# Twenty-four weight-sum stores move from SyncE's DMA queue to GpSimd's beside the first MoE's paired blocks

## The chip, the cores and the metric

The kernel runs on one core of one Trainium2 chip. The metric is the device time of one execution in microseconds (us), compared as the median of several runs. The engines are named as in the profile: PE (TensorE), DVE (VectorE), ACT (ScalarE), POOL (GpSimd) and SP (SyncE, which only issues DMAs here). "SPq" is SP's sequencer.

## The reference, cut to what matters

Three stages follow one another over 3072 tokens of width 512: chunked attention with memory tokens, a gated MLP ("MoE 1", d_ff 1536) and a second MLP ("MoE 2", d_ff 2048). Weights and activations are float32.

```python
def _moe_ref(x, w_gate, w_val, w_out, rms_g):
    rms = np.sqrt(np.mean(x * x, axis=-1, keepdims=True) + 1e-06)
    xn = x / rms * rms_g
    g = xn @ w_gate
    silu = g * (1.0 / (1.0 + np.exp(-g)))
    return (silu * (xn @ w_val) @ w_out).astype(np.float32)

def _moe2_ref(x, w_in, w_out):
    h = x @ w_in
    g = np.where(h >= 1.0, h, np.where(h <= -1.0, 0.0, (h + 1.0) ** 2 / 4.0))
    return (g @ w_out).astype(np.float32)
```

## The kernel before, in words

A float32 product is made of three fp32r matmuls (high x high, high x low, low x high), so every operand is split into a high part (an ACT copy to fp32r) and a low part (a DVE subtraction).

The six token tiles of 512 are treated in two ways. The first four go through MoE 1 one at a time (the "single" part, up to about 487 us), while attention for the later tiles runs in between. The last two go through MoE 1 together as a pair, and then MoE 2 takes all six tiles as three pairs. For a pair, a 2x2 block product is done with 7 products of sub-blocks instead of 8 (Strassen's scheme, in `seven`). That needs, beside the raw weight blocks, four sums and differences of weight blocks for each group of weights. These are prepared once, in the background, split into high and low parts, and stored to DRAM in `w1p_d`, `w1o_d` (MoE 1) and `w2p_d`, `w2o_d` (MoE 2), from where the pair stages load them again.

The background work is a list of small steps, `bg`, taken off by `conv_step`. For MoE 2, `w2_steps(g)` handles one group of four weight blocks in 28 steps:

- `load_w2` loads a raw 512 KB block `w` through POOL's queue (line 274). It takes one of three buffers, so it waits until an earlier block's stores have landed.
- `c`, `join`, `hi`, `lo` turn the 64-bit words into float32 and split them (ACT line 287, DVE lines 144 and 145, ACT line 290, DVE line 293). `lo` stores the split blocks through POOL's queue (line 301).
- `pair_sums` makes two sums of two blocks (DVE lines 196 to 200). Then `hi_s` (ACT line 203) and `lo_s` (DVE line 206) split each, and `lo_s` stores the two parts with two DMAs of 256 KB each (line 208), all on SP's queue.

The sums stand in the tiles `late`, two of them in turn; the high part overwrites one of the float32 blocks (`tu` or `g_b`).

In the pair stage of MoE 1 the loop `for f in range(F1)` (12 blocks) calls `proj1`, and that calls `seven`: seven `product`s of 6 matmuls each. After product i, SP is told to load the weights of product i + 14 into the 14 slots of `wp` (part of the tile `wall`, line 807). Background steps are called between the products. ACT and DVE move the sums of products between the PSUM banks and make the activations.

The order of all instructions on all engines is written out by hand here (`manual_schedule`). Each engine takes its instructions in program order: a DMA that waits for its data holds up everything behind it on the same engine.

`m2["single"]` is true until the single part is over. It is set to False just before the pair stage of MoE 1, after the background sums in progress have been finished.

Of the kernel before, what the change touches and what calls it, by code (L numbers as in the profile page):

```python
# [39 lines left out]
def tile_stream_attention_moe_moe2(  # L40
# [10 lines left out]
    nc = tc.nc  # L51
# [153 lines left out]
    def lo_s(S, k, h, dst):  # L205
        tt_(out=flat(S[k]), in0=flat(S[k]), in1=h.bitcast(F32), op=ALU.subtract)
        for n, src in enumerate((h.bitcast(F32), flat(S[k]))):
            nc.sync.dma_start(dst(n, k), src.rearrange("p (k c) -> p k c", k=2))

    def in_dst(dp):  # L210
        return lambda n, k: dp[:, 3 + 2 * k:5 + 2 * k, n]
# [14 lines left out]
    def sum_steps(i, srcs, raws, order, dst):  # L226
        n = 8 * i
        h, S = [], []

        def whole():  # L230
            if i % 2:
                h.extend(tmp.tile([P, 512], U32, tag="tu", name="wgv") for _ in range(2))
            else:
                gv = wst.tile([P, 1024], U32, tag="w64", name="wgv")
                h.extend([gv[:, :512], gv[:, 512:]])
            for x, w in zip(h, srcs):
                tt_(out=x.bitcast(F32), in0=w[:, 0], in1=w[:, 1], op=ALU.add)

        def first():
            S.extend(halves(wst.tile([P, 1024], F32, tag="w64", name="s1234")))  # L240
            sums(S, *order(h), True)

        at(n, lambda: (nc.gpsimd.dma_start(*raws[0]), whole()))
        at(n + 1, first)
        at(n + 2, lambda: sums(S, *order(h), False))
        for k, r in enumerate(raws[1:]):
            at(n + 2 + 2 * k, lambda r=r: nc.gpsimd.dma_start(*r))
        at(n + 4, lambda: hi_s(S, 0, h[0]))
        at(n + 5, lambda: hi_s(S, 1, h[1]))
        at(n + 6, lambda: lo_s(S, 0, h[0], dst))  # L250
        at(n + 7, lambda: lo_s(S, 1, h[1], dst))
# [26 lines left out]
    def w2_steps(g):  # L278
# [38 lines left out]
        def pair_sums(a, b, n, order, dst):  # L317
            S, h = [], lambda: (f32_[a], f32_[b])

            def first():  # L320
                if m2["single"]:
                    S.extend([sp.tile([P, TT], F32, tag="s", name="s12"), sums_.tile([P, TT], F32, tag="s34", name="s34")])
                else:
                    S.extend(m2["late"][a // 2 % 2][:, i] for i in range(2))
                S[:] = [x.rearrange("p (k c) -> p k c", k=2) for x in S]
                live.append(a)
                sums(S, *order(h()), True)

            at(n + 10, first)
            at(n + 11, lambda: sums(S, *order(h()), False))  # L330
            at(n + 13, lambda: hi_s(S, 0, f32_[a]))
            at(n + 14, lambda: hi_s(S, 1, f32_[b]))
            at(n + 15, lambda: lo_s(S, 0, f32_[a], dst))
            at(n + 16, lambda: (lo_s(S, 1, f32_[b], dst), live.remove(a)))
# [4 lines left out]
    m2 = {"single": True, "pace": 0.0, "hold": False}  # L339
# [302 lines left out]
    for st in ORDER.split():  # L642
        c, n = st[0], st[1:]
# [3 lines left out]
        n = int(n)  # L647
# [26 lines left out]
        elif c == "L":  # L674
            dst, hi = (x[:, :, n * P:n * P + P] for x in (xl, xh))
# [631 lines left out]
```

## Time and profile before

| | us |
|---|---|
| median of 3 runs | 1133.96 |
| lowest and highest run | 1133.13, 1137.2 |
| the profiled execution's own time | 1134.45 |
| its span in the trace | 1132.7 |

The span runs from the first to the last instruction of the trace; the execution's own time holds 1.75 us more around it. Times in the trace count from the start of the span. The page gives busy time by engine; queries of the trace give it by stretch of time, and what each instruction waited for. The stretch that the change touches is the pair stage of MoE 1, from 486.9 to 601.2 us.

### The profile page before, as it was taken

The page shows a single profiled execution, that of the slowest core. Times are in us where ns is not written, and L with a number is a line of the kernel's source. Part 1 is how long each engine was busy: PE and PEld are TensorE (multiplying, and loading weights), DVE is VectorE, ACT ScalarE, POOL GpSimd, SP SyncE. Part 2 cuts the span into 40 slices and gives each one's busy share as a digit, 9 for nine tenths or more (in the row PEclk, how much of TensorE's full clock was granted, in tenths as well). Part 3 has the DMA queues.
Part 4 walks back from the last instruction along what each step waited for, and adds up shares of the span by engine and source line. Part 5 has one row for each costly group of instructions (what it writes and reads, how often), then busy time and mean ns, then how long its engine had stood idle before and what let it go on. Part 6 is the DMA issues. An engine that isn't in the chain of part 4 may idle for free.

```text
span 1132.7 us, 20941 instructions
## 1 busy us (share of the span) xinstructions
PE 1113.5 (98%) x7882; PEld 911.7 (80%) x7882; DVE 817.4 (72%) x1433; ACT 617.1 (54%) x1089; POOL 102.8 (9%) x152
## 2 busy tenths in 40 slices
PE   6999999999999999999999999999999999999998
PEld 4777888888888888788888888888888888888886
DVE  4987666777666766666767867897678987578855
ACT  3887655666567765534445544466344565344553
POOL 0200003221222122111110000000000000000000
PEclk6999999999999999999999999999999999999999
DMA  8967259998878976899997798756778666762564
GB/s 281 359 232 256 87 187 298 299 349 291 286 248 288 299 261 220 291 320 382 404 390 223 217 318 259 202 182 199 234 205 268 186 190 219 221 197 83 168 193 159
DMA packets 144212, 281.81 MB, mean 249 GB/s; under 512 B 15216, under 2 KB 65392, under 8 KB 142320
## 3 DMA queue, kind: packets, MB, share of 16 engines
q1 hardware_dynamic: 123936, 228.83, 62.3%
q0 software_dynamic: 12768, 43.52, 11.2%
q10 hardware_dynamic: 7408, 8.13, 2.1%
q8 instruction: 62, 1.02, 0.4%
q14 instruction: 38, 0.31, 0.1%
HBM read 201.26 MB, written 79.17 MB: 248 GB/s over the span
## 4 chain that ended last, share of the span: by engine, by line
PE 92%; DVE 3%; ACT 2%; DMA 1%; issue 1%; SPq 0%; POOL 0%; DVEq 0%; ACTq 0%; POOLq 0%
PE ps_y L1085 14%; PE ps_g L1085 11%; PE ps_g L567 7%; PE ps_g L569 7%; PE ps_g L568 7%; PE ps_b L903 4%; PE ps_b L905 4%; PE ps_b L904 4%; PE ps_g L903 4%; PE ps_g L905 4%; PE ps_g L904 4%; PE ps_y L567 4%; PE ps_y L569 3%; PE ps_y L568 3%; PE ps_y L903 2%; PE ps_y L905 2%
## 5 line engine op out<-in xcount | busy, mean ns | idle before, releaser
L1085 PE MATMUL ps_y<-r,wo 128*128 128x512 f32 x672 | 156.7, 391 | 0.0
L567 PE MATMUL ps_g<-xh,wall 128*128 128x512 f32 x380 | 151.8, 399 | 1.2 <-ACT s L866 0.7
L569 PE MATMUL ps_g<-xh,wall 128*128 128x512 f32 x380 | 148.5, 391 | 1.0 <-DVE wall L160 1.0
L568 PE MATMUL ps_g<-xl,wall 128*128 128x512 f32 x380 | 148.3, 390 | 0.0
L1085 PEld LDWEIGHTS ps_y<-r,wo 128*128 128x128 f32 x672 | 125.6, 188 | 26.6 <-DVE r L1024 0.8
L1024 DVE TENSOR_TENSOR r<-h,r 128x512 fp32r<-128x512 f32 x155 | 103.9, 689 | 44.3 <-ACT r L1022 44.3
L975 ACT ACTIVATE t<-t,half 128x512 f32<-128x512 f32 x96 | 66.9, 720 | 122.7 <-DVE t L974 122.7
L1022 ACT ACTIVATE r<-h 128x512 fp32r<-128x512 f32 x155 | 93.1, 625 | 56.2 <-DVE r L1024 17.5
L1085 PE MATMUL ps_g<-r,wo 128*128 128x512 f32 x498 | 116.0, 390 | 0.0
L1085 PEld LDWEIGHTS ps_g<-r,wo 128*128 128x128 f32 x498 | 93.2, 188 | 19.3 <-DVE r L1024 0.2
L567 PEld LDWEIGHTS ps_g<-xh,wall 128*128 128x128 f32 x380 | 71.3, 188 | 17.9 <-ACT s L866 1.2
L569 PEld LDWEIGHTS ps_g<-xh,wall 128*128 128x128 f32 x380 | 71.4, 188 | 16.5 <-DVE wall L160 1.4
L568 PEld LDWEIGHTS ps_g<-xl,wall 128*128 128x128 f32 x380 | 71.4, 188 | 13.8
L903 PE MATMUL ps_b<-wall 128*128 128x512 f32 x202 | 78.8, 390 | 0.0
L905 PE MATMUL ps_b<-wall 128*128 128x512 f32 x202 | 78.7, 390 | 0.0
L904 PE MATMUL ps_b<-wall 128*128 128x512 f32 x202 | 78.7, 389 | 0.0
L903 PE MATMUL ps_g<-wall 128*128 128x512 f32 x198 | 77.4, 391 | 0.0
L905 PE MATMUL ps_g<-wall 128*128 128x512 f32 x198 | 77.1, 390 | 0.0
L904 PE MATMUL ps_g<-wall 128*128 128x512 f32 x198 | 77.1, 390 | 0.0
L567 PE MATMUL ps_y<-hh,wall 128*128 128x512 f32 x192 | 76.7, 399 | 0.0
L568 PE MATMUL ps_y<-hl,wall 128*128 128x512 f32 x192 | 75.1, 391 | 0.0
L569 PE MATMUL ps_y<-hh,wall 128*128 128x512 f32 x192 | 75.0, 391 | 0.0
(209 smaller groups left out, 2101.9 us busy)
## 6 DMA issues: line engine op xcount, KB each, us to landing
wo<-w2o_d SPq DMA_DIRECT2D x88, 512.0 KB, 3.5
wall<-w2p_d SPq DMA_DIRECT2D x168, 256.0 KB, 3.1
wall<-w1p_d SPq DMA_DIRECT2D x84, 256.0 KB, 6.3
w<-in_w_dram POOLq DMA_DIRECT2D x32, 512.0 KB, 5.6
w<-in_w_dram SPq DMA_DIRECT2D x30, 512.0 KB, 5.2
k_in<-in_k_dram SPq DMA_DIRECT2D x48, 256.0 KB, 5.1
wo<-w1o_d SPq DMA_DIRECT2D x21, 512.0 KB, 3.7
v_in<-in_v_dram SPq DMA_DIRECT2D x40, 260.0 KB, 5.1
```

The source lines that it names most:

```text
L567: nc.tensor.matmul(ps, wh, xh, start=start, stop=False)
L568: nc.tensor.matmul(ps, wh, xl, start=False, stop=False)
L569: nc.tensor.matmul(ps, wl, xh, start=False, stop=stop)
L903: nc.tensor.matmul(bank, wh, xh, start=st, stop=False, skip_group_check=True)
L904: nc.tensor.matmul(bank, wh, xl, start=False, stop=False, skip_group_check=True)
L905: nc.tensor.matmul(bank, wl, xh, start=False, stop=kk == 1, skip_group_check=True)
L975: nc.scalar.activation(s, s, AF.Square, scale=0.5, bias=half)
L1022: nc.scalar.activation(r[:, 0], src, AF.Copy)
L1024: tt_(out=r[:, 1], in0=src, in1=r[:, 0].bitcast(F32), op=ALU.subtract)
L1085: nc.tensor.matmul(bank[p][m], a, b, start=s0, stop=s1, skip_group_check=True)
```

## The change

`lo_s`, which stores the parts of a weight sum, chooses its queue: SP while `m2["single"]` is true, as before, and GpSimd afterwards. Everything else stays as it was, so the stores of line 208 that fall in the pair stage of MoE 1 are issued by POOL, and SP's queue holds loads only there.

```diff
     def lo_s(S, k, h, dst):
         tt_(out=flat(S[k]), in0=flat(S[k]), in1=h.bitcast(F32), op=ALU.subtract)
         for n, src in enumerate((h.bitcast(F32), flat(S[k]))):
-            nc.sync.dma_start(dst(n, k), src.rearrange("p (k c) -> p k c", k=2))
+            queue = nc.sync if m2["single"] else nc.gpsimd
+            queue.dma_start(dst(n, k), src.rearrange("p (k c) -> p k c", k=2))
```

## Rows read from the trace of the kernel before

**Rows 1.** The page, busy time of each engine, share of the span, instructions.

```profile
PE 1113.5 (98%) x7882; PEld 911.7 (80%) x7882; DVE 817.4 (72%) x1433; ACT 617.1 (54%) x1089; POOL 102.8 (9%) x152
```

**Rows 2.** Busy time by stretch: before, in and behind the pair stage.

```profile
core 0: us, PE busy (x) PEld busy (x) DVE busy (x) ACT busy (x) POOL busy (x), PEclk, DMA share, GB/s
487.20:601.20 114.00, 114.00 (x505) 94.36 (x504) 72.92 (x130) 48.13 (x88) 17.98 (x27) 1.00 1.03 382
601.20:640.00 38.80, 38.80 (x173) 32.15 (x172) 33.05 (x48) 24.22 (x41) 0.00 (x0) 1.00 0.64 191
```

**Rows 3.** PE's waits from 440 to 640 us: sum, times, longest.

```profile
PE ps_g L567 <- DVE s L875: 0.4, 1, 0.4
```

**Rows 4.** PE in order of time: the stage's first and last matmul.

```profile
486.91 0.39 PE L903 MATMUL ps_g<-wall 128*128 128x512 f32 x1
...
600.95 0.39 PE L905 MATMUL ps_g<-wall 128*128 128x512 f32 x1
```

**Rows 5.** Line 208 from 480 to 610 us: semaphore events, time to landing.

```profile
L208 SPq EVENT_SEMAPHORE  x24: 17/17/17, 501.1 to 593.2; - x24
...
DMA to landing us min/median/max: 4.5/6.2/11.5
```

**Rows 6.** SP's queue in order of time, where it lags most.

```profile
552.18 0.37 SPq L208 DMA_DIRECT2D w2o_d<-tu  x1
554.07 0.37 SPq L208 DMA_DIRECT2D w2o_d<-late  x1
557.53 0.33 SPq L807 DMA_DIRECT2D wall<-w1p_d  x1
...
561.74 0.98 SPq L807 DMA_DIRECT2D wall<-w1p_d  x2
```

**Rows 7.** Line 807, the product weights, from 487 to 602 us: landing.

```profile
DMA to landing us min/median/max: 2.8/6.3/11.7
```

**Rows 8.** POOL in order of time; in brackets its idle time before.

```profile
497.92 0.71 POOL L301 DMA_DIRECT2D w2p_d<-w  x1
504.09 0.58 POOL L274 DMA_DIRECT2D w<-in_w_dram  x1 [5.46 <-DMA w2p_d<-w]
...
514.70 1.42 POOL L301 DMA_DIRECT2D w2o_d<-w  x2 [2.24 <-DVE w L293]
521.55 0.55 POOL L274 DMA_DIRECT2D w<-in_w_dram  x1 [5.43 <-DMA w2o_d<-w]
...
560.10 0.55 POOL L274 DMA_DIRECT2D w<-in_w_dram  x1 [9.28 <-DMA w2o_d<-w]
```

**Rows 9.** DVE in order of time: two of line 206's twelve instructions.

```profile
502.44 0.69 DVE L206 TENSOR_TENSOR late<-late,tu 128x512 f32<-128x512 f32 x1
...
514.94 0.69 DVE L206 TENSOR_TENSOR late<-late,g_b 128x512 f32<-128x512 f32 x1
```

**Rows 10.** Line 301, POOL's own stores, 470 to 610 us: issue in ns, landing.

```profile
L301 POOL DMA_DIRECT2D w2p_d<-w x9: 707/707/803, 489.0 to 569.0; - x9
L301 POOL DMA_DIRECT2D w2o_d<-w x9: 707/717/728, 504.9 to 588.9; - x9
...
DMA to landing us min/median/max: 4.7/6.6/9.3
```

**Rows 11.** Line 274, the raw loads, 470 to 610 us: landing.

```profile
DMA to landing us min/median/max: 4.0/6.5/8.2
```

**Rows 12.** ACT in order of time: line 287 uses the raw blocks.

```profile
514.81 0.65 ACT L287 ACTIVATE tu<-w 128x512 f32<-128x512 f32 x1
...
569.23 0.65 ACT L287 ACTIVATE tu<-w 128x512 f32<-128x512 f32 x1
...
571.93 0.42 ACT L290 ACTIVATE w<-tu 128x256 fp32r<-128x256 f32 x1 [1.53 <-issue]
```

**Rows 13.** Line 144 on DVE, 487 to 602 us: min, median, max ns.

```profile
L144 DVE TENSOR_SCALAR tu<-tu x8: 419/421/483, 491.9 to 570.7; 128x512 uint32<-128x512 uint32 x8
```

**Rows 14.** DMA queues, 487.2 to 601.2 us: packets, MB, share of 16 engines.

```profile
q1 hardware_dynamic: 19873, 34.00, 80.8%
q0 software_dynamic: 2736, 9.44, 21.8%
```

## The prediction

> **What bounds the kernel now.** I read the page's busy times first: PE is busy for 98% of the span, no other engine for more than 72% [rows 1]. That is an average, so the next view is the stretch that the change touches. Line 208 issues 24 stores from 501.1 to 593.2 us, all inside MoE 1's pair stage [rows 5]. The busy times by stretch show PE at 114.00 of 114.00 us there, at the full granted clock, and at 38.80 of 38.80 us behind it [rows 2]. Since a busy PE need not be PE at its peak, I counted as well. The stage has 12 x 7 products of 6 matmuls, that is 504; from the first one's start to the last one's start lie 600.95 - 486.91 = 114.04 us, or 114.04 / 503 = 0.227 us for each matmul [rows 4], with no gap left over. The view of waits agrees: from 440 to 640 us PE waits once, for 0.4 us [rows 3], and that wait comes before the stage, at line 567. So PE's rate sets the end of this stage, and whatever the change frees on SP can at best be cover that PE does not need. The reader should also see in [rows 2] that the DMA engines are busy throughout (share 1.03, 382 GB/s). They are the second limit, and the place where a loss could come from.
>
> **The change part by part.**
>
> *SP loses 24 stores.* What SP lost to them is best seen at its worst place: after a store at 552.18 it issues one load of product weights, at 557.53, and the next at 561.74 [rows 6], while PE finishes a product every 6 x 0.227 = 1.36 us and so frees about 7 slots. SP is thus late by some 8 us, because a store waits in order and so do the loads behind it. What would that have cost? A load goes out when product i is done and is used by product i + 14, so 13 products lie between: 13 x 1.36 = 17.7 us. The landing takes 6.3 us in the median, 11.7 at most [rows 7]. Late by 8 and landing in 6.3 makes 14.3, under 17.7; and PE shows no wait. With the stores gone the lag goes, and the cover grows by up to 8 us. Worth in time: 0. The most that it could be worth is PE's whole idle time around the stage, 0.4 us [rows 3].
>
> *POOL gains 24 stores.* POOL's own stores of the same size (256 KB) take 0.707 to 0.717 us each to issue [rows 10]. 24 x 0.71 = 17.0 us, so POOL goes from 17.98 to about 35 of 114 us [rows 2]; it does no other work that anyone waits for in the stage. What counts is its order. Behind each new store stand the next raw load (line 274) and the next store of a block (line 301). They come in six pairs of sums, four stores each; I show the first, which is the tightest, and the second, where POOL is busy itself when the sums are ready.
>
> First pair: line 301 is issued at 497.92. The last of the four stores needs line 206 of DVE, which ends at 502.44 + 0.69 = 503.13 [rows 9] (its high part was ready before, since line 206 reads it). The store so ends at 503.13 + 0.71 = 503.84. The raw load behind it goes at 504.09 today, because it waits for the store of 497.92 to land [rows 8]. Margin 0.25 us.
>
> Second pair: POOL is busy with two stores from 514.70 to 516.12 [rows 8]; line 206 ends at 514.94 + 0.69 = 515.63 [rows 9], so all four are ready and end at 516.12 + 4 x 0.71 = 518.96. The next raw load goes at 521.55. Margin 2.6 us.
>
> So the new stores fill time in which POOL waits for a landing anyway (5.46 and 5.43 us of idle time in these rows). A late raw load would have cover too. The one of 504.09 is used on ACT at 514.81, 10.7 us later; the tightest of the eight from there on is that of 560.10, used at 569.23, 9.1 us later [rows 8, 12]. They land in 6.5 us in the median and 8.2 at most [rows 11], which leaves 2.6 us or more at the median and 0.9 at the longest. Behind line 287 ACT has idle time too, 1.53 us before line 290 at 571.93 [rows 12]. Cost: 0.
>
> *The transfers themselves.* The same 24 x 256 KB = 6.3 MB move, on another queue. Does a byte cost more there? In the stage POOL's queue moved 9.44 MB for 21.8% of the engines, 43.3 MB for 100%; SP's 34.00 MB for 80.8%, 42.1 MB for 100% [rows 14]. Landing takes 6.6 us for POOL's stores and 6.2 for SP's [rows 5, 10]. From below: the queue change gives nothing back, as PE does not wait. From above: if landings grew by the 0.4 us between these medians, the cover above would take it. I take 0.
>
> [...] POOL's store issues keep within 0.707 and 0.803 us although DVE is busy for 72.92 of the 114 us [rows 2, 10]; on the other side the fastest pass over 512 columns on DVE, line 144, is 0.421 us in the median and 0.483 at most [rows 13], so neither holds the other up by more than about 0.1 us. [...]
>
> **The sum.** 0 (SP) + 0 (POOL) + 0 (transfers) against the profiled execution's own time of 1134.45 us, whose span is 1132.7 us. That execution lies 0.5 us above the median of the runs shown, 1133.96 us, so I forecast 1134.0 us.
>
> **The rivals.**
>
> *Slower: GpSimd's queue becomes the wait.* Place: the raw load behind each set of stores. If the new stores held each of the eight loads back by as much as a whole landing, 6.5 us, the first would be in place 6.5 + 6.5 - 10.7 = 2.3 us late for ACT and the tightest 6.5 + 6.5 - 9.1 = 3.9 us, 3.1 between them. ACT takes its work in order, and the moves between PSUM banks that PE needs stand behind it; ACT's idle time of 1.53 us comes off, so PE loses 1.6 us, eight times 12.8 us: 1147 us. It passes 0.5% (5.7 us, or 0.7 us for each load) once the loads are held back by 5.6 us each. That takes about 1.4 us more for each store of four than the 0.71 us that the rows show. Against it: 18 issues at 0.71 us. [...]
>
> *Slower: the transfers interleave worse.* The DMA engines are busy all through the stage. If the moved 6.3 MB cost as much again, 6.3 MB / 382 GB/s = 16 us more transfer time would fall into 114 us, and less whatever the weight loads' cover of 17.7 us takes up: between 0 and 16 us. Against it: both queues move a byte for the same share [rows 14], and the loads' landing has 6 us of room even at its longest.
>
> *Faster: SP's release shortens the stage.* For it: the 8 us lag of SP. Against it: PE has only 0.4 us to give; 1133.6 us, which cannot be told from no change.
>
> *It does not do what it says.* Ruled out by reading: `single` is False from before the first of the 24 stores, and they are the only ones of line 208 behind it.
>
> **How the numbers follow.** A measurement of this kernel can tell about 0.5% (5.7 us) from no change. No change: 0.94. GpSimd's queue: 0.03; by half its price or less it would still lie within 0.5%. Transfers: 0.01. A gain over 0.5%: 0.02, for which the trace shows no source. So faster 0.02, same 0.94, slower 0.04. The range: below, the lowest run 1133.13 less PE's 0.4 us and as much again for scatter, 1132.4; above, the highest run 1137.2 and a small part of the first rival, 1138.0.
>
> **What would show it.** Right: in the changed kernel 24 DMA issues of line 208 stand on POOL between about 498.6 and 592 us, POOL's busy time in the stage is near 35 us, SP's queue shows the product-weight loads in an even row, and PE is still busy for 114.0 of 114 us. Wrong: line 287 waits on ACT for a raw block, POOL's issues take more than 1 us, landings of line 807 come near 17 us, or the matmuls of lines 903 to 905 show any idle time before them. If PE's time in the stage changes with none of these, the matmul rate itself depends on the transfers, which nothing here shows.

## The result: slower, and the profile after

The changed kernel takes 1144.12 us (median of 5 runs, 1142.33 to 1146.63) against 1133.96 us before. The ratio is 1.0087, with a 95% interval of 1.0073 to 1.01. The forecast was 1134.0 us within 1132.4 to 1138.0, and no change with a chance of 0.94. It was wrong. The lines of the changed file below 208 stand one further on: the stores are line 209 now, the raw loads 275, the block stores 302, ACT's use of the raw blocks 288, the matmuls 904 to 906.

The page's busy times by engine, changed kernel:

```profile
PE 1116.4 (98%) x7882; PEld 913.1 (80%) x7882; DVE 817.6 (71%) x1433; ACT 618.4 (54%) x1089; POOL 120.8 (11%) x176
```

At this level nothing can be seen: PE is at 98% as in [rows 1], and POOL has 24 instructions and 18.0 us more, 17.0 of which were forecast. The busy times by stretch show where to look:

```profile
487.20:601.20 114.00, 105.98 (x464) 86.43 (x463) 70.18 (x126) 46.05 (x83) 31.68 (x47) 1.00 0.98 355
```

PE was busy for 114.00 of these 114 us before [rows 2], now for 105.98, at the same granted clock. In order of time PE's first matmul of the stage and the first one behind the stage are:

```profile
489.69 0.39 PE L904 MATMUL ps_g<-wall 128*128 128x512 f32 x1
```

```profile
613.17 1.07 PE L1086 MATMUL ps_y<-r,wo 128*128 128x512 f32 x4
```

613.17 - 489.69 = 123.48 us. Before, the stage took 114.26 us (from 486.91 [rows 4] to the first matmul behind it, at 601.17). So this stage loses 9.2 us, where the medians lie 10.2 us apart. Its start, 2.8 us later in this execution, is no part of it: the first moved store goes at 501.51 us, and among the other runs whose program is the same up to there (before, e3, e4, e8) the start lies anywhere between 485.2 and 488.6 us.

PE's waits from 440 to 660 us, where there was one of 0.4 us [rows 3]:

```profile
PE ps_b L904 <- ACT ps_b L928: 2.9, 1, 2.9
PE ps_g L904 <- ACT ps_g L928: 2.4, 1, 2.4
PE ps_g L904 <- DVE ps_b L938: 1.9, 1, 1.9
PE ps_g L904 <- DVE ps_y L938: 0.8, 1, 0.8
```

PE waits for the moves between PSUM banks, 8.0 us in sum. The other 1.1 us lie at the first matmuls behind each wait, which follow each other more slowly than the rest (565.91 to 566.25, so 0.34 us, where 0.227 is usual). The four waits come at 552, 556, 566 and 599 us; up to 550 us PE loses nothing. What held the moves up stands in ACT's waits, of which none for a raw block was listed in this stage before:

```profile
ACT tu L288 <- DMA w<-in_w_dram: 11.3, 4, 6.0
...
ACT g_b L288 <- DMA w<-in_w_dram: 9.0, 3, 4.5
```

The longest, in ACT's order of time:

```profile
562.32 0.67 ACT L288 ACTIVATE tu<-w 128x512 f32<-128x512 f32 x1 [6.04 <-DMA w<-in_w_dram]
...
565.27 0.59 ACT L928 ACTIVATE ps_b<-ps_b 128x512 f32<-128x512 f32 x1
```

And the matmul that waits for the last of these, in PE's order:

```profile
565.91 0.50 PE L904 MATMUL ps_b<-wall 128*128 128x512 f32 x1 [2.86 <-ACT ps_b L928]
```

This is the chain that the first rival named: a raw block comes late, ACT waits for it in order, and the move of line 928 behind it is late for PE. The raw block of this wait was loaded at 550.90 and took 11.3 us to land, where 8.2 us was the most before [rows 11], so not all of the 6.04 us comes from a late issue. Why the raw blocks are issued late can be read on POOL. In order of time, the first two sets of stores and a later load; in brackets the idle time before:

```profile
500.22 0.55 POOL L275 DMA_DIRECT2D w<-in_w_dram  x1 [6.97 <-DMA w2p_d<-w]
500.81 0.71 POOL L302 DMA_DIRECT2D w2p_d<-w  x1
501.51 0.72 POOL L209 DMA_DIRECT2D w2p_d<-tu  x1
502.23 0.72 POOL L209 DMA_DIRECT2D w2p_d<-late  x1
507.81 0.72 POOL L209 DMA_DIRECT2D w2p_d<-tu  x1 [4.86 <-ACT g_b L288]
...
509.41 0.58 POOL L275 DMA_DIRECT2D w<-in_w_dram  x1
...
518.43 1.42 POOL L302 DMA_DIRECT2D w2o_d<-w  x2
519.85 0.71 POOL L209 DMA_DIRECT2D w2o_d<-tu  x1
525.37 0.73 POOL L209 DMA_DIRECT2D w2o_d<-late  x1 [4.81 <-issue]
...
528.04 0.55 POOL L275 DMA_DIRECT2D w<-in_w_dram  x1
530.52 0.72 POOL L302 DMA_DIRECT2D w2p_d<-w  x1 [1.93 <-DVE h L953]
...
540.48 0.55 POOL L275 DMA_DIRECT2D w<-in_w_dram  x1 [8.10 <-DMA w2p_d<-w]
```

Each store is issued in 0.71 to 0.73 us, as forecast. But in each of the first five sets one store stands still for 4.8 us or more with POOL free; in the first two it is the third at 507.81 and the second at 525.37. The view guesses a releaser (ACT) or finds none ("issue"). The time tells more. The block store issued three DMAs before, at 500.81, has this time to landing:

```profile
DMA to landing us min/median/max: 6.7/6.7/6.7
```

So it landed at 507.5; the waiting store goes 0.3 us after that. At 571.30 it is the same: the block store of 564.17 took 6.8 us, landed at 571.0, and again 0.3 us later the store goes. The next raw load stands behind the waiting store. Before, it went 504.09 - 497.92 = 6.2 us after the block store of its set, and 521.55 - 514.70 = 6.9 us in the second set [rows 8]; now 509.41 - 500.81 = 8.6 and 528.04 - 518.43 = 9.6 us. Behind the raw load the next block stores now wait too (530.52).

By the cover that the prediction counted (2.6 us or more at the median landing) a delay of some 2.5 us in one set should cost nothing, but the delays add up. A raw load waits for the landing of an earlier block's store, and that block came late already. Counted from the start of the stage, the second load of the stage (509.41, before 504.09) is 2.5 us later than before. The fifth is 540.48 - 489.69 = 50.79 us behind the start, where it was 531.15 - 486.91 = 44.24 us, so 6.6 us later; the wait for its block is the first that ends in a wait of PE, at 552 us. Before:

```profile
531.15 0.55 POOL L274 DMA_DIRECT2D w<-in_w_dram  x1 [7.50 <-DMA w2p_d<-w]
```

Before, the blocks from the second load on had landed 2.7 to 4.8 us before ACT used them. Now it is 0.8 us for the second, and from the third on ACT takes each within 0.1 us of its landing.

SP did what was forecast. Its queue in order of time shows one even row where it had lagged [rows 6], and no gain came of it:

```profile
551.92 40.49 SPq L808 DMA_DIRECT2D wall<-w1p_d  x28
```

### The profile page after: what moved, and what is told of

Its sections match the earlier page's. It is cut to its first block, busy times and chain, and to the rows that moved or that the text cites. A ratio compares the mean times of both kernels' runs of the same rounds, so it can differ in the third digit from the quotient of the medians.

```text
span 1144.8 us, 20943 instructions
## 1 busy us (share of the span) xinstructions
PE 1116.4 (98%) x7882; PEld 913.1 (80%) x7882; DVE 817.6 (71%) x1433; ACT 618.4 (54%) x1089; POOL 120.8 (11%) x176
## 4 chain that ended last, share of the span: by engine, by line
PE 83%; DMA 7%; DVE 3%; ACT 3%; issue 2%; POOL 1%; SPq 0%; POOLq 0%; ACTq 0%; DVEq 0%
PE ps_y L1086 14%; PE ps_g L1086 11%; PE ps_g L568 6%; PE ps_g L569 6%; PE ps_g L570 6%; PE ps_b L904 4%; PE ps_b L906 3%; PE ps_b L905 3%; DMA w<-in_w_dram 3%; PE ps_g L904 3%; PE ps_y L568 3%; PE ps_g L906 3%; PE ps_g L905 3%; PE ps_y L569 3%; PE ps_y L570 3%
```

## The experiments

Two theories were to be told apart. **Ring:** GpSimd's DMAs take up a room of fixed size until they have landed; a DMA for which there is no room waits, and all behind it on POOL. **Crowding:** SP's loads, no longer held up by stores, take the DMA engines from the raw loads. The stage times below run from the first matmul of lines 904 to 906 to the first one behind the stage (114.26 us before, 123.48 us after).

**e1: twice the room.** The launch of the kernel has a number that may be that room.

```diff
-    nc = _bacc.Bacc("TRN2", ..., dynamic_dma_scratch_size=1024)
+    nc = _bacc.Bacc("TRN2", ..., dynamic_dma_scratch_size=2048)
```

> [...] To find the room, the last of MoE 1's 36 weight units shares the buffer of unit 27 (so MoE 1's block 9 is computed with other weights after the first tile), MoE 1's pair uses 7 instead of 8 ring tiles and 6 instead of 7 steps of lead for its output blocks, and MoE 2 has 6 instead of 7 scratch tiles; e2 has the same with 1024 bytes. Ring theory (a DMA on GpSimd's queue waits until earlier ones have landed, because their descriptors fill the room; in the changed kernel each set's third store goes 0.3 us after the landing of the DMA three before it): twice the room lets all four stores of a set go as soon as data and GpSimd are ready; PE needs 114.3 us for the stage's 504 matmuls again, ACT's waits for raw blocks (20.3 us in the changed kernel) fall under 3 us, and the time lies some 9 us under that of e2. Crowding theory (SP's loads, no longer held up by stores, take the DMA engines from the raw loads): as e2, stage 122 to 124 us. [...]

**e2: its control.** e1's other edits alone:

```diff
-    wall2 = poolS("wall2", 1).tile([P, 15, 2, 512], F32R, name="wall2")
+    wall2 = poolS("wall2", 1).tile([P, 14, 2, 512], F32R, name="wall2")
...
-    second_pool(F1 // 2, 5, 5, "ring t wo h")
+    second_pool(F1 // 2, 4, 5, "ring t wo h")
...
-    second_pool(G2, 5, 7, "wo t ring c h")
+    second_pool(G2, 5, 6, "wo t ring c h")
```

> [...] All theories: the stage takes 122 to 124 us as in the changed kernel (123.5), and the third store of each set waits 4.8 to 6 us on GpSimd. The total may differ from the changed kernel's 1144 us by a few us, since the fewer tiles touch other stages.

The fewer weight buffers make one block of MoE 1 compute with other weights in both kernels; the stage has 504 matmuls in both.

Measured: e1 takes 1136.23 us (ratio to before 1.0019, 1.0007 to 1.0031), e2 1144.19 us (1.0094, 1.0075 to 1.0113). The stage takes 603.74 - 488.65 = 115.09 us in e1 and 609.15 - 486.39 = 122.76 us in e2. PE in order of time, the first matmuls behind the stage, in e1:

```profile
603.74 5.60 PE L1086 MATMUL ps_y<-r,wo 128*128 128x512 f32 x24
```

and in e2:

```profile
609.15 5.60 PE L1086 MATMUL ps_y<-r,wo 128*128 128x512 f32 x24
```

POOL's second set in e1, in order of time:

```profile
517.00 1.42 POOL L302 DMA_DIRECT2D w2o_d<-w  x2
518.41 0.71 POOL L209 DMA_DIRECT2D w2o_d<-tu  x1
519.11 0.72 POOL L209 DMA_DIRECT2D w2o_d<-late  x1
519.83 0.71 POOL L209 DMA_DIRECT2D w2o_d<-g_b  x1
520.52 0.72 POOL L209 DMA_DIRECT2D w2o_d<-late  x1
524.08 0.55 POOL L275 DMA_DIRECT2D w<-in_w_dram  x1 [2.83 <-DMA w2o_d<-w]
```

Here all four stores go one behind the other, ending 518.41 + 4 x 0.71 = 521.2 us, as the prediction had worked it out for the kernel before; the raw load goes 7.1 us after the block stores and waits for their landing alone. The stores, their engine, VectorE's work and SP's freedom are those of e2. So the room is the cause, and crowding is not needed for more than the 0.8 us that e1's stage is still over 114.26.

That e2's stage is as long as the changed kernel's is in part chance. PE waits twice in e2, 2.5 and 2.1 us, in place of 8.0 us in sum. The other 122.76 - 114.26 - 4.6 = 3.9 us lie in matmuls that follow each other more slowly. The granted clock, in the third column from the right, is 0.97 over 114 us of the stage in e2:

```profile
487.20:601.20 114.00, 109.42 (x467) 89.31 (x466) 71.51 (x128) 45.22 (x82) 33.80 (x49) 0.97 0.99 358
```

By an estimate from this row the clock costs 0.03 x 114 = 3.4 us. In the changed kernel and in e1 it is 1.00 over the same 114 us. So between e1 and e2 the room is worth waits of 4.6 us, and with them the time of a lower clock.

**e3: the stores on ACT's queue.**

```diff
-            queue = nc.sync if m2["single"] else nc.gpsimd
+            queue = nc.sync if m2["single"] else nc.scalar
```

> The stores of the pair stage's weight sums are issued by ACT instead of GpSimd; SP issues loads only, as in the changed kernel. Ring theory: GpSimd's queue is as before the change, so the raw loads come in time: stage 114.3 us, total within 3 us of the kernel before, plus what ACT loses by waiting in order for line 206 (12 times, up to about 1 us each; part of it idle time anyway). Crowding theory: SP is as free as in the changed kernel, so the raw loads are as late: stage 120 us or more, total 1140 us or more. [...]

Measured: 1143.23 us (1.0078, 1.0057 to 1.0098), stage 612.14 - 488.55 = 123.59 us. The ring theory's number was missed, by another wait. The raw loads were in time: no wait of ACT for them in the stage, landing 6.4 us in the median with SP's queue as free as in the changed kernel, which speaks against crowding once more. ACT now waits at its own stores (ACTq is its sequencer):

```profile
539.97 0.37 ACTq L209 DMA_DIRECT2D w2p_d<-late  x1
540.39 0.60 ACT L960 ACTIVATE t<-ps_b 128x512 f32<-128x512 f32 x1 [5.08 <-DMA wo<-w1o_d]
```

Line 206 on DVE had the data of the store at 539.97 ready at 536.75 + 0.69 = 537.44. The store went 2.5 us later, and the view puts ACT's 5.08 us of idle time down to the landing of a load that SP had issued. There are three such waits, 5.1, 2.8 and 7.0 us, and PE waits 5.6 us for ACT's moves. The other 123.59 - 114.26 - 5.6 = 3.7 us lie in slower matmuls: the granted clock is 0.97 from 487.2 to 601.2 us, as in e2. Why a store of ACT should wait for SP's transfers was not tried.

**e4: half of the stores.** The high parts stay on GpSimd, the low parts go back to SP.

```diff
-            queue = nc.sync if m2["single"] else nc.gpsimd
+            queue = nc.sync if m2["single"] or n else nc.gpsimd
```

> Of the 24 moved stores the 12 of the high parts stay on GpSimd, the 12 of the low parts go back to SP. Ring theory: with two stores in a set, a raw load, a block store and the two stores fit together, so nothing waits for room in the sets behind one block store, and in those behind two block stores one store waits: less than a third of the loss is left, stage 114.3 to 117 us, total 1134 to 1137 us. [...]

Measured: 1133.5 us (0.9998, 0.9986 to 1.0009), stage 599.53 - 485.21 = 114.32 us, no wait of PE. In POOL's order of time the set behind one block store does not wait for room, the one behind two does, as expected:

```profile
497.27 0.71 POOL L302 DMA_DIRECT2D w2p_d<-w  x1
497.97 0.72 POOL L209 DMA_DIRECT2D w2p_d<-tu  x1
499.73 0.72 POOL L209 DMA_DIRECT2D w2p_d<-tu  x1 [1.04 <-ACT tu L203]
...
512.96 1.47 POOL L302 DMA_DIRECT2D w2o_d<-w  x2 [1.12 <-DVE w L294]
514.43 0.71 POOL L209 DMA_DIRECT2D w2o_d<-tu  x1
519.45 0.72 POOL L209 DMA_DIRECT2D w2o_d<-g_b  x1 [4.32 <-issue]
520.83 0.55 POOL L275 DMA_DIRECT2D w<-in_w_dram  x1 [0.65 <-DMA w2o_d<-w]
```

The wait of 4.32 us costs nothing, nor does one of 8.16 us in the fourth set: each is over before the raw load behind it could have gone. Half the stores cost none of the loss, not half of it: with 12 of them on GpSimd the stage takes 114.32 us, with 24 it takes 123.48.

**e5: stores of one run.** Is the room counted in DMAs or in pieces? The sums are laid out so that a store writes one run of 2 KB for each partition.

```diff
-        return lambda n, k: dp[:, 3 + 2 * k:5 + 2 * k, n]
+        return lambda n, k: pair_(dp, 3 + 2 * k)[:, 512 * n:512 * n + 512].rearrange("p (a c) -> p a c", a=2)
...
-        return lambda n, k: do[:, (1, 4)[k]:(3, 6)[k], u, n]
+        return lambda n, k: pair_(do, (1, 4)[k])[:, 512 * (2 * u + n):512 * (2 * u + n) + 512].rearrange("p (a c) -> p a c", a=2)
```

(`pair_` takes two neighbouring blocks as one flat run; `load_wp` and `load_wo` read the sums as two runs.)

> The changed kernel with the weight sums laid out so that each store writes one contiguous run of 2 KB for each partition instead of two of 1 KB; the loads of the sums read two runs of 1 KB in turn. All results are still computed. The number of stores, their bytes and their queue stay. Ring theory, room counted in pieces: a block store of two runs takes twice as much as a store of one run, so a raw load, a block store and four stores fit, and only in the sets behind two block stores one store waits: stage 114.3 to 117 us, time 1134 to 1137 us. Ring theory, room counted in DMAs (a fixed number in flight, whatever their size): as in the changed kernel, stage 122 to 124 us, time 1143 to 1146 us. [...]

Measured: 1137.09 us (1.0021, 1.0005 to 1.0036), stage 603.69 - 488.40 = 115.29 us. POOL in order of time; the block stores are line 309 here:

```profile
535.22 0.71 POOL L309 DMA_DIRECT2D w2p_d<-w  x1
535.92 0.58 POOL L209 DMA_DIRECT2D w2p_d<-tu  x1
...
537.59 0.54 POOL L209 DMA_DIRECT2D w2p_d<-late  x1
...
551.49 1.45 POOL L309 DMA_DIRECT2D w2o_d<-w  x2
552.93 0.56 POOL L209 DMA_DIRECT2D w2o_d<-tu  x1
553.47 0.55 POOL L209 DMA_DIRECT2D w2o_d<-late  x1
560.77 0.54 POOL L209 DMA_DIRECT2D w2o_d<-g_b  x1 [6.75 <-issue]
```

The same number of stores with the same bytes: behind one block store all four now go at once, behind two the third waits, both as expected from counting pieces. A fixed number of DMAs in flight is ruled out.

**e6 and e7: three quarters of the room, for the changed kernel and for the kernel before.**

```diff
-    nc = _bacc.Bacc("TRN2", ..., dynamic_dma_scratch_size=1024)
+    nc = _bacc.Bacc("TRN2", ..., dynamic_dma_scratch_size=768)
```

> [...] Ring theory: two stores of two runs fit in place of three, so the second store of a set waits already, and the next block stores too; the stage becomes longer than the changed kernel's 123.5 us, some 130 us or more. Earlier stages may lose time as well, since MoE 1's own block stores go by the same queue from 170 to 300 us. [...]

> [...] Ring theory: in the pair stage a raw load and two block stores still fit, so the stage stays at 114.3 us with PE never waiting, while the same cut costs the changed kernel several us there. [...]

Measured: e6 takes 1152.43 us (two runs; 1.0156, 1.0121 to 1.019), stage 621.62 - 487.44 = 134.18 us; e7 takes 1133.5 us (0.999, 0.9979 to 1.0), stage 600.83 - 486.26 = 114.57 us. The same cut costs the changed kernel 10.7 us in the stage and the kernel before 0.3. In e6 PE waits 14.0 us, 6.0 more than in the changed kernel (its two longest waits are 6.9 and 4.9 us); the other 4.7 us of the 10.7 lie in matmuls that follow each other more slowly. In e6 the second store of a set waits already, in POOL's order of time:

```profile
499.54 0.72 POOL L302 DMA_DIRECT2D w2p_d<-w  x1
500.25 0.72 POOL L209 DMA_DIRECT2D w2p_d<-tu  x1
505.62 0.72 POOL L209 DMA_DIRECT2D w2p_d<-late  x1 [4.65 <-DVE w L294]
```

**e8: the raw loads on SP, all stores on GpSimd.**

```diff
-            nc.gpsimd.dma_start(w2raw[j], wts2[4 * g + (0, 2, 1, 3)[k]].bitcast(U32))
+            (nc.gpsimd if m2["single"] else nc.sync).dma_start(w2raw[j], wts2[4 * g + (0, 2, 1, 3)[k]].bitcast(U32))
```

> The changed kernel with the raw loads of line 275 issued by SP in the pair stage; all stores of the stage stay on GpSimd. Ring theory: stores still wait on GpSimd, but the raw loads no longer stand behind them; they wait only for their buffer, that is for the landing of block stores which themselves may wait for room. Most of the loss goes: stage 114.3 to 118 us, time 1134 to 1138 us. SP waits in order for these buffers and its product weights come later, within their 17.7 us of cover. Crowding theory: raw loads as late as before or later, stage 122 us or more.

Measured: 1136.39 us (1.0017, 1.0007 to 1.0027), stage 602.43 - 485.74 = 116.69 us, PE waits 1.4 us. The raw loads' landing was as long as in the changed kernel (7.5 against 7.4 us in the median, 6.5 before [rows 11]), and all stores of the stage stand on GpSimd's queue as there, yet most of the loss is gone. So it is for the most part the place of the loads behind the waiting stores that costs the time, not their longer way. The 2.4 us that are left are not taken apart here.

## Why the prediction was wrong, point by point

**What bounds the kernel: right.** PE sets the end of the stage; the stage lost what PE waited and what the first matmuls behind the waits took longer.

**SP loses 24 stores, worth 0: right.** Its row of loads is even and nothing was gained.

**POOL gains 24 stores, cost 0: this is the step that failed.** The walk over POOL's rows let a store go as soon as POOL was free and its data ready. It had the issue time right (0.71 us) and POOL's busy time within a microsecond (18.0 us more against 17.0). It left out a third condition, room for what is in flight, so that "margin 0.25 us" and "margin 2.6 us" stood where a wait of 4.8 us or more falls. In e1, where there is room, the second set goes as the walk had it: its four stores end 4.2 us behind the issue of the block stores, by the walk 518.96 - 514.70 = 4.3. Measured, the step costs 9.2 us. A second thing failed with it: the walk took the cover of each raw load to stand anew in each set. In fact the 2.5 us of the first set were not made good, and from the third load on no cover was left.

The waits fit an account by pieces, an estimate from these traces alone. Count a DMA by its contiguous runs for each partition: a raw load or a one-run store of e5 is 1 piece, a block store or a store of two runs 2. In the changed kernel a raw load, a block store and two stores (7 pieces) are in flight together; a third store (9) waits, still with the load landed (8), and goes with the block store landed too (6). That is the wait seen, for the block store three DMAs before. So the room is put at 7 pieces with the number 1024, by proportion at 14 with 2048 and 5.25 with 768. The 13 pieces of e1's second set go without a wait. One-run stores fit behind one block store, all four of them (7), and behind two the third does not (8), e5. With 768 the second store of a set does not fit (7, e6); a load and two block stores would (5), and in e7 PE never waits. Every set shown above agrees. Followed through this stage in the traces of before and of the changed kernel, POOL never has more than 7 pieces in flight, and where this room is what a DMA waits for, it goes some 0.3 us after the landing that makes it. What one piece takes up no run here shows.

**The transfers themselves, cost 0: nearly right.** POOL's stores of the sums landed in 5.3 us in the median, no later than SP's had [rows 5]. The raw loads took 7.4 us instead of 6.5 [rows 11]; one took 11.3, and PE's wait at 566 us hangs on it. In e8 they took as long and the stage lost 2.4 us, so this alone costs at most that.

**DVE's work beside POOL's issues: as read.** The issue times stayed at 0.71 to 0.73 us with DVE busy for 70.18 of the 114 us, and e1 gives nearly all of the loss back with the same stores on the same engine (stage 115.09 us).

**The first rival: right in place, wrong in cause and chance.** It named the raw load behind each set, ACT's order and PE's wait, at 1147 us; it came out at 1144.12. It asked for about 1.4 us more for each store, so that each load is held back by at least 5.6 us. What came was one wait of some 5 us in each set, of which the load behind it lost 2.4 and 2.7 us in the first two; by the rival's sum, which takes each load by itself, that would have cost nothing. The loss came because the delays added up, in four waits of PE from 552 us on. That the 1147 us lie near the measured time is luck. Its chance of 0.03 rested on 18 issues of a stretch in which POOL never had more in flight than a raw load and two block stores. A stretch in which it had more was in the trace of before, outside the stage that I read. POOL in order of time, kernel before, storing MoE 1's blocks:

```profile
246.33 0.74 POOL L247 DMA_DIRECT2D w1o_d<-wall  x1
247.07 0.72 POOL L243 DMA_DIRECT2D w1p_d<-wall  x1
247.79 0.73 POOL L247 DMA_DIRECT2D w1p_d<-wall  x1
250.80 0.72 POOL L247 DMA_DIRECT2D w1p_d<-wall  x1 [2.28 <-issue]
...
254.75 0.73 POOL L247 DMA_DIRECT2D w1p_d<-wall  x1 [1.78 <-issue]
```

The stores go in threes (the second is that of 250.80, 251.52 and 252.25), with a pause behind each three for which the view finds no cause. That was the row to price the new stores by.

**A version better than both** did not come out of it: e4 and e7 measure the same as the kernel before, since PE has nothing to give in this stage.

## What to carry to other kernels

When a DMA moves to another engine's queue, ask not only whether that engine is free but how much it may have in flight: look in the whole trace for the longest burst that the queue ever issued, and at pauses behind it that have no releaser. Here room on GpSimd's queue goes by pieces, so one contiguous run for each partition (e5, stage 115.29 us), half the stores (e4, 114.32) or a larger room (e1, 115.09) each gave back all or nearly all of the 9.2 us. And in an in-order queue the price of a wait is set by what stands behind it: here the loads, which with the stores' wait ahead of them cost 9.2 us and on another queue (e8) 2.4. Where those loads wait for buffers that the delayed work itself frees, ask whether the cover is there again in the next round: here 2.5 us late became 6.6 us by the fifth load.

## What was not expected of the hardware

With the launch's number at 1024, three 256 KB stores of two runs are what GpSimd's queue issues in a row at 246.33 and at 250.80 us of the kernel before, with pauses of 2.28 and 1.78 us behind them, and in the changed kernel a waiting DMA goes 0.3 us after the landing that makes room (507.5 to 507.81, 571.0 to 571.30). A store on ACT's queue can be held as well: in e3 ACT idled 5.1, 2.8 and 7.0 us at its stores, by the view until transfers that SP had issued landed, and the stage came out as long (123.59 us) as with the waits on GpSimd; its cause stays open. And a wait of PE need not cost its own length alone: with waits of 4.6 us in sum in e2 and 5.6 in e3 the granted clock over 114 us of the stage was 0.97, and the matmuls took 3.9 and 3.7 us more besides; with waits of 8.0 us in the changed kernel it was 1.00, and they took 1.1 us more.
